# Strassen's products for half of h in two more chunks of a fused attention and MLP kernel, with a newer order of operations and column halves that shift the instruction stream

## The chip, the cores and the metric

The kernel runs on one core of a Trainium2 chip (trn2). The metric is device time in microseconds (us) of that core; the span in a profile is some 1.8 us shorter than the time of the same execution. Every kernel here gave correct results against the reference.

## The reference

Linear attention with a cosine weighting, 8 batches of 8 heads, 576 positions, head size 64, followed by a two-layer MLP whose activation is h / (1 + exp(-beta h)):

```python
q_p, k_p = phi(q, cos_w, sin_w), phi(k, cos_w, sin_w)        # relu, times cos and sin
kv  = einsum('bhsf,bhsd->bhfd', k_p, v);  z = k_p.sum(axis=2)
num = einsum('bhsf,bhfd->bhsd', q_p, kv)
x   = num / (einsum('bhsf,bhf->bhs', q_p, z)[..., None] + 1e-6)   # then to (4608, 512)
h   = x @ w_in                                               # 512 -> 2048
out = (h / (1 + exp(-beta * h))) @ w_out                     # 2048 -> 512
```

## The kernel before

The 4,608 tokens go in nine chunks (0 to 8) of 512. A chunk computes h, the activation and the output products, and the attention of the next batch is woven between them. Every chunk's h has 16 tiles of 128 features. From chunk 2 on the output product uses seven products of half size in place of eight (Strassen's scheme in Winograd's form). From chunk 5 on half of the h tiles do so too, in four pairs X, Y, Z, V:

```python
def h_fast(c, jt0, banks):                      # one pair of h tiles: 7 products, 2 matmuls of 256 columns each
    "1": prod(b_ps, w(0, 0), x(0, 0), ...)      # "5" needs t1, "6" t2, "7" t3, "4" t4: the sums of x
    "5": prod(e_ps, s1, t1, ...)                # s1..s4: the sums of the weights (wh_sums)
    ...
def wh_sums(jt):                                # 4 subtractions or additions on DVE, 128x256
def x_sums(c):                                  # 4 on DVE, 128x512

def num_mm(b, n, jp, bank, slot):               # 8 matmuls 64x65; a batch's numerator is 144 of them in one go
...
FAST = 5
for c in range(2, NTC):                         # chunks below FAST: plain h, then the output products
    x, y = o_fast(c, 0, xb, cols[0]), o_fast(c, 1, yb, cols[1])
    if c >= FAST:
        chunk(c, b, x, y, parts)                # follows a list of operations, ORDER
        continue
    sums = h_first(c)                           # 16 plain tiles
    for t, bank in enumerate(parts): num_all(b, t, bank)     # the numerator's burst
    for i, n in enumerate("156273"):            # output products, with the divisions x_part between them
        ...
        x_part(b, i, parts[i])                  # part 0 frees bank 6, which product "2" writes
```

A "numerator burst" below is that run of 144 tiny matmuls and 144 weight loads between a chunk's h and its output products.

## Time and profile before

| | before |
|---|---|
| time, median of the first 3 runs | 282.33 us (280.57 to 282.58) |
| span of the profiled run | 279.65 us, clock 1.000 |
| TensorE (PE) busy | 272.2 us, 97% |
| DVE / ACT / GpSimd busy | 209.1 / 177.8 / 71.9 us |
| matmul instructions | 3,592 records on the chip |

Read it from PE: it is busy nearly all the time, so what counts is the work in its queue and the few places where it stops. The prediction below shows those places. A table of stretches by chunk gives the scale. The columns are stretch, its length, and then each engine's busy time with its number of instructions, the granted clock, the DMA share and GB/s. The stretches run from the first output product of one chunk to that of the next, for chunks 2 to 6:

```profile
98.22:127.64 29.42, 28.94 (x396) 19.51 (x392) 17.17 (x48) 19.93 (x37) 9.01 (x10) 1.00 0.85 214
127.64:156.40 28.76, 28.76 (x403) 19.43 (x392) 21.81 (x69) 19.93 (x37) 9.06 (x10) 1.00 0.83 203
156.40:184.90 28.50, 28.15 (x425) 21.82 (x416) 22.40 (x60) 21.50 (x46) 9.06 (x10) 1.00 0.66 163
184.90:213.10 28.20, 28.20 (x497) 24.74 (x483) 22.84 (x61) 21.23 (x46) 8.94 (x10) 1.00 0.30 61
```

The last stretch holds a Strassen h (chunk 6), the first two plain ones (chunks 3 and 4). The stretches get shorter by tenths, not by microseconds.

### The profile page before, as it was taken

How to read it: one execution, taken by the hardware profiler on the slowest of the kernel's cores; microseconds unless marked ns; L12 is line 12 of the kernel's file. 1: busy time of each engine (PE TensorE's matmuls, PEld its weight loads, DVE VectorE, ACT ScalarE, POOL GpSimd, SP SyncE). 2: the span in 40 equal slices, each digit the busy share in tenths (PEclk: the TensorE clock that was granted, in tenths of full speed). 3: DMA queues.
4: the chain of work that ended last, by engine and by line, in shares of the span. 5: the costliest groups of instructions: out<-in, count | busy, mean ns of one | idle time of the engine just before them, and what ended most of it. 6: DMA issues, size and time to landing. Idle time of an engine off the chain costs nothing.

```text
span 279.6 us, 8687 instructions
## 1 busy us (share of the span) xinstructions
PE 272.2 (97%) x3592; PEld 192.4 (69%) x3592; DVE 209.1 (75%) x539; ACT 177.8 (64%) x348; POOL 71.9 (26%) x89
## 2 busy tenths in 40 slices
PE   8999999999999999999999999999999999999993
PEld 8564455455674588548854886679888886888783
DVE  5989967669999586357749977799679779649832
ACT  5778756772137557675757585896685179529911
POOL 1444000633194074106320542007400140000000
PEclk9999999999999999999999999999999999999999
DMA  7999999999979959992899289407400540033006
GB/s 243 373 394 385 391 390 323 348 244 397 164 233 330 293 151 249 182 340 41 196 193 374 61 205 250 177 12 115 116 1 7 122 113 1 2 79 74 0 2 150
DMA packets 50583, 53.98 MB, mean 193 GB/s; under 512 B 31200, under 2 KB 31472, under 8 KB 50544
## 3 DMA queue, kind: packets, MB, share of 16 engines
q1 hardware_dynamic: 47584, 45.82, 58.0%
q0 software_dynamic: 2688, 7.34, 9.2%
q8 instruction: 28, 0.46, 0.7%
q10 hardware_dynamic: 272, 0.27, 0.4%
q14 instruction: 11, 0.09, 0.2%
HBM read 36.71 MB, written 9.44 MB: 165 GB/s over the span
## 4 chain that ended last, share of the span: by engine, by line
PE 89%; DMA 5%; DVE 3%; issue 1%; ACT 0%; ACTq 0%
PE ps L544 30%; PE ps L378 22%; PE ps L472 11%; PE ps L521 8%; PE ps L426 7%; DMA raw_q<-in_q_dram 5%; PE ps L293 4%; PE ps L272 3%; PE ps L602 1%; PE ps L234 1%; PE ps L606 1%; DVE xs L315 1%; DVE vb L219 0%; PE ps L616 0%; PE ps L352 0%
## 5 line engine op out<-in xcount | busy, mean ns | idle before, releaser
L378 PE MATMUL ps<-xt,win 128*128 128x512 bf16 (+1 forms) x324 | 71.1, 377 | 0.1
L386 ACT ACTIVATE g_t<-ps,beta 128x512 bf16<-128x512 f32 x80 | 54.6, 688 | 19.2 <-PE ps L378 17.9
L378 PEld LDWEIGHTS <-win 128*128 128x128 bf16 x324 | 31.1, 98 | 35.4 <-issue 0.2
L514 POOL DMA_DIRECT2D out_dram<-o_sb x56 | 32.7, 590 | 66.6 <-DVE o_sb L595 34.3
L544 PEld LDWEIGHTS <-S 128*128 128x128 bf16 x469 | 44.2, 98 | 4.8
L417 ACT ACTIVATE g_t<-ps,beta 128x512 bf16<-128x512 f32 x64 | 41.2, 696 | 3.4 <-PE ps L426 2.2
L544 PEld LDWEIGHTS <-g_t 128*128 128x128 bf16 x357 | 32.9, 98 | 3.7
L222 POOL TENSOR_TENSOR qs<-qt,tanr 128x1152 bf16<-128x1152 bf16 x8 | 18.9, 2387 | 48.5 <-DVE S L397 17.6
L397 DVE TENSOR_TENSOR S<-g_t 128x512 bf16<-128x512 bf16 (+1 forms) x62 | 22.3, 393 | 11.5 <-ACT g_t L386 9.1
L521 PE MATMUL ps<-wout,g_t 128*128 128x512 bf16 (+1 forms) x158 | 29.2, 339 | 0.0
L544 PE MATMUL ps<-wout,g_t 128*128 128x256 bf16 (+1 forms) x231 | 28.1, 270 | 0.0
L544 PE MATMUL ps<-wout,S 128*128 128x256 bf16 (+1 forms) x238 | 27.4, 266 | 0.0
L544 PE MATMUL ps<-T,S 128*128 128x256 bf16 (+1 forms) x231 | 27.1, 269 | 0.0
L426 PE MATMUL ps<-xt,win 128*128 128x512 bf16 (+1 forms) x120 | 24.0, 336 | 0.0
L315 DVE TENSOR_TENSOR xs<-ps,rden 128x768 bf16<-128x768 f32 (+4 forms) x26 | 22.8, 883 | 0.8
L219 DVE TENSOR_SCALAR vb<-raw_v,cos 128x256 bf16<-128x256 f32 x63 | 22.9, 421 | 0.2 <-DMA raw_v<-in_v_dram 0.2
L521 PEld LDWEIGHTS <-g_t 128*128 128x128 bf16 x158 | 15.0, 98 | 11.0
L217 ACT ACTIVATE vb<-raw_v,sin 128x256 bf16<-128x256 f32 (+1 forms) x50 | 21.8, 499 | 0.8 <-DMA raw_v<-in_v_dram 0.8
L472 PE MATMUL ps<-w_stage 128*128 128x256 bf16 x120 | 20.3, 273 | 0.4 <-DVE w_stage L458 0.4
L472 PEld LDWEIGHTS <-w_stage 128*128 128x128 bf16 x160 | 15.5, 98 | 4.2 <-issue 0.5
L222 POOL TENSOR_TENSOR w_stage<-qt,tanr 128x1152 bf16<-128x1152 bf16 x4 | 9.5, 2380 | 26.1 <-DVE den L304 26.1
L426 PEld LDWEIGHTS <-win 128*128 128x128 bf16 x120 | 11.7, 98 | 6.3
(104 smaller groups left out, 384.9 us busy)
## 6 DMA issues: line engine op xcount, KB each, us to landing
raw_v<-in_v_dram SPq DMA_DIRECT2D x7, 1152.0 KB, 10.9
raw_k<-in_k_dram SPq DMA_DIRECT2D x7, 1152.0 KB, 8.4
raw_q<-in_q_dram SPq DMA_DIRECT2D x7, 1152.0 KB, 7.8
out_dram<-o_sb POOLq DMA_DIRECT2D x56, 128.0 KB, 5.2
w_stage<-in_moe_w_in_dram SPq DMA_DIRECT2D x3, 1024.0 KB, 13.3
w_stage<-in_moe_w_out_dram SPq DMA_DIRECT2D x2, 1024.0 KB, 8.4
w_stage<-in_moe_w_out_dram SPq DMA_DIRECT2D x4, 512.0 KB, 12.0
out_dram<-o_sb SPq DMA_DIRECT2D x13, 128.0 KB, 2.4
```

The costliest lines, as they stand in the source:

```text
L219: nc.vector.tensor_scalar(o, a, scalar1=t[:, n : n + 1], scalar2=None, op0=ALU.mult)
L222: return eng.tensor_tensor(dst.rearrange("q n (g p) -> q n g p", g=2), src.rearrange("q n (g p) -> q n g p", g=2), tanr[:, n0:n1].unsqueez ...
L315: nc.vector.tensor_tensor(o.rearrange("q j n s d -> q j (n s) d"), nv[:, :, a:z, :, 0:D].rearrange("q j n s d -> q j (n s) d"), rden[:, :, ...
L378: nc.tensor.matmul(ps[:, h_bank(c, jt), blocks.start * 64 : blocks.stop * 64], lhsT=win[jt // 4][:, mi, (jt % 4) * P : (jt % 4 + 1) * P], ...
L386: nc.scalar.activation(gs[c, jt // 4][:, jt % 4], ps[:, h_bank(c, jt)], AF.Silu, scale=beta[:, jt : jt + 1])
L397: return nc.vector.tensor_tensor(o, l, r, op=op)
L417: nc.scalar.activation(gs[c, jt // 4][:, jt % 4], ps[:, bank], AF.Silu, scale=beta[:, jt : jt + 1])
L426: nc.tensor.matmul(ps[:, bank, o * 64 : z * 64], lhsT=win[jt // 4][:, mi, (jt % 4) * P : (jt % 4 + 1) * P], rhs=xt[:, o:z, jp, g * HP : (g ...
L472: nc.tensor.matmul(dst, lhsT=left[:, g], rhs=right[:, :, g * HP : (g + 1) * HP], start=start and g == 0, stop=stop and g == 1, skip_group_ ...
L514: eng.dma_start(out=out_v[bb, n][:, m0:m1], in_=o_sb[hf * HP : (hf + 1) * HP, m0:m1])
L521: nc.tensor.matmul(o_ps[:, m0 : m0 + w], lhsT=gs[c, jt // 4][:, jt % 4, tt * P : (tt + 1) * P], rhs=wout[:, jt, m0 : m0 + w], start=(jt == ...
L544: nc.tensor.matmul(dst[:, m : m + w], lhsT=left(i), rhs=right[:, i, m : m + w], start=start and i == 0, stop=stop and i == order[-1], skip ...
```

## The change

Its intent: Strassen's products for half of h already from chunk 3, with a newer order of operations in those chunks, the weight sums of the four pairs moved into chunk 2 (those of the last chunk's two further pairs into chunk 6), and matmuls split in two column halves at chosen places. A split does the same work with two instructions more (a weight load and a matmul), so it moves all later instructions of PE's stream. The core of the diff:

```diff
-    def h_mm(c, jt, mis=range(4), blocks=slice(0, NB)):
+    def h_mm(c, jt, mis=range(4), blocks=slice(0, NB), cols=1):      # cols=2: two halves
...
-            o_part(1, (slot - 16) // 4, slot % 4, 2 if slot > 23 else 1)
+            o_part(1, (slot - 16) // 4, slot % 4, 2 if slot > 18 else 1)
...
-    H_COLS, O_COLS = {6: 8}, {5: ("4", "25734")}
+    SPLITS = {2: (6, 9), 3: (8, 10), 4: (7, 10), 5: (5, 0)}   # chunk: h tiles in halves, last output products in halves
...
-            if c == FAST - 1 and slot in (2, 4, 6, 8, 10, 12):
-                wh_sums((0, 4, 8, 12, 2, 6)[slot // 2 - 1])
+            if slot in (10, 12, 14):
+                for jt in ((0, 4), (8,), (12,))[slot // 2 - 5]:
+                    wh_sums(jt)
...
-    FAST = 5
+    FAST = 3
...
     (in the output products of the last plain chunk)
-        v_half(b + 1, 0, 0, 3)
+        v_half(b + 1, 0, 0, 5)
         y["5"]()
         y["c5"]()
+        if c == FAST - 1:
+            x_sums(c + 1)
...
-    ORDER = ("Y1 c1Y X5 X1 ... p3 q0 sp4 ... cuV q1 p5 ...
+    ORDER = ("p0 Y1 X1 c1X ... oy6 w8 q0 q1 cuy ...          (another order; q0, q1 far later)
```

## The prediction

> **What bounds the kernel now.** I read the page's busy shares first, then PE's own waits, the timeline around each of them, and a table of stretches by chunk.
>
> ```profile
> PE 272.2 (97%) x3592; PEld 192.4 (69%) x3592; DVE 209.1 (75%) x539; ACT 177.8 (64%) x348; POOL 71.9 (26%) x89
> ...
> PEclk9999999999999999999999999999999999999999
> ...
> PE ps L602 <- DVE zero_b L149: 1.0, 1, 1.0
> PE ps L293 <- issue: 0.9, 2, 0.5
> PE ps L293 <- ACT kv L282: 0.5, 1, 0.5
> PE ps L472 <- DVE w_stage L458: 0.4, 1, 0.4
> PE ps L234 <- DVE qb L194: 0.2, 1, 0.2
> ```
>
> TensorE is busy 97% at full clock and its listed waits come to 3.0 us: only fewer columns, or those few waits, can shorten the span of 279.6 us. The starts of successive matmuls lie 216 ns apart at 512 columns, 109 ns at 256 and 55 to 56 ns at 128 (medians over the trace). Two of the waits concern this change. The "issue" wait:
>
> ```profile
> 97.42 0.22 PE L293 MATMUL ps<-kv,qt 64*64 64x65 bf16 x4
> 98.06 0.23 PE L293 MATMUL ps<-kv,qs 64*64 64x65 bf16 x4 [0.43 <-issue]
> ...
> 126.72 0.22 PE L293 MATMUL ps<-kv,qt 64*64 64x65 bf16 x3
> 127.42 0.19 PE L293 MATMUL ps<-kv,qt 64*64 64x65 bf16 x1 [0.48 <-issue]
> ```
>
> The attention numerator is a burst of 144 tiny matmuls with 144 weight loads, 288 instructions in about 1.27 us. In chunk 2 (96.24 to 98.07) and chunk 3 (125.61 to 127.52) it takes 1.83 and 1.91 us from first to last start; in chunks 4 and 6 it takes 1.24 and 1.30. The excess is 1.20 us. Counted in PE's own stream, the two gaps stand at instructions 2755 and 3522, 767 apart, which is three blocks of 256 less one. The queue of instruction fetches moved 28 packets of 16 KB for PE's roughly 7,200 instructions, one per 256. Those fetches start at 95.50 and 125.01 us, 2.4 to 2.6 us before the gap ends. So I read a gap as PE reaching the end of a block before the next has arrived. The second wait, at L472, is chunk 5's first Strassen product behind the sums of x:
>
> ```profile
> 168.64 0.38 PE L472 MATMUL ps<-xt,win 128*128 128x256 bf16 x2
> ...
> 168.90 0.42 DVE L458 TENSOR_TENSOR w_stage<-xt 128x512 bf16<-128x512 bf16 x1
> ...
> 169.37 0.38 PE L472 MATMUL ps<-w_stage 128*128 128x256 bf16 x2 [0.35 <-DVE w_stage L458]
> ```
>
> Start to start it costs 0.5 us more than the 0.22 that two products need.
>
> [...]
>
> **The change part by part.** *Strassen in chunks 3 and 4.* Eight pairs more. A pair of plain tiles is 8 matmuls of 512 columns, 8 x 216 = 1.728 us; by products it is 14 of 256, 14 x 109 = 1.526. Eight pairs save 1.62 us of PE, on the path. ACT and DVE get four pairs' copies and adds more per chunk, about 6.8 us on DVE (16 x 0.42) and 3.0 on ACT (8 x 0.38). Chunk 5 already runs so, with 22.4 us of DVE and 21.6 of ACT in 28.6, and PE stood only in the wait above. I take chunks 3 and 4 to be like it: no new wait.
>
> *Column halves.* The built program has 3,871 matmuls against 3,589. Strassen makes 8 x (14 - 8) = 48 of the 282, so 234 are net splits at about 2.5 ns: 0.59 us lost. As a check, chunk 5's output products before ran 154 matmuls in 12.44 us where chunk 7's 112 took 12.33: 42 splits, 0.11 us, 2.6 ns each. What they are for shows when the block ends are counted in both built streams. Within the 288 instructions, the later block end of chunks 2 to 6 lay before at place 280, 263, 246, 181, 240, and lies after at 206, 223, 232, 253, 188. Two of those before stalled, at 280 and 263; none did at 246 or below, beyond 0.06 at 240. [...] I expect both gaps to go, 1.20 us, and something between 0 and 0.5 to appear in chunk 5 at 253, where I interpolate 0.2 us.
>
> *Sums of x placed earlier.* The first Strassen chunk's sums of x now stand inside the second half of chunk 2's output products, some 4 us ahead of their use: the 0.5 us wait goes.
>
> *Sums of the weights.* Four of the six, 16 operations at about 0.23 us of pitch (0.93 for four in the timeline of chunk 4), move from chunk 4 into the last third of chunk 2's h. This is the part that I distrust. DVE there before:
>
> ```profile
> 91.94 0.70 DVE L284 CAST kv<-ps 128x520 bf16<-128x520 f32 x1 [1.34 <-PE ps L272]
> 93.61 0.76 DVE L397 TENSOR_TENSOR S<-g_t 128x512 bf16<-128x512 bf16 x2 [0.97 <-ACT g_t L386]
> ...
> 98.01 0.16 DVE L304 TENSOR_TENSOR den<-ps,eps 128x12 f32<-128x12 f32 x1
> ...
> 100.85 1.04 PE L544 MATMUL ps<-wout,g_t 128*128 128x256 bf16 x8
> ```
>
> After the cast at 91.94 DVE idles 0.97, 0.17 and 0.70 us, 1.84 in all, and the new sums need 16 x 0.23 = 3.7. Laid end to end: eight sums to 94.4, the g sums to 95.9, four to 96.9, g sums to 97.9, four to 98.9, the last g sums to 99.85, then the first division (1.42 us) to 101.27 in place of 99.43. That division frees bank 6, which output product 2 must write. Product 2 began at 100.85, and without the fetch gap would begin at 100.25: PE then waits about 1.05 us. Later adds run late too, and I give 0.1 to product 4 of the second half. Cost 1.15 us.
>
> Sum: 1.62 + 1.20 + 0.5 gained, 0.59 + 1.15 + 0.2 lost, net 1.4 us.
>
> **The rivals.** (a) *DVE keeps up in chunk 2*, because PE is itself later or the sums run tighter: net 2.5 us, time near 279.5. For it: chunk 4 took 24 such operations without a PE wait. Against it: chunk 4 spread them over seven slots and had no k, v and q work in its h; chunk 2 has 13.6 us of DVE work in 16.95 already. (b) *Chunks 3 and 4 stand on new waits*, since their DMA queues are fuller: the mean DMA share is 0.85 and 0.82 in the stretches of chunks 2 and 3 against 0.66 in chunk 4's, and the transposes of x must land before the sums of x. For it: the transposes of q take 11.4 us to land (median). Against it: no wait of PE on a DMA is listed after the start, and the new order puts the q work after the x transposes. It would eat 0.5 to 2 us: 281 to 283. (c) *The fetch gaps only move*, to other blocks or to chunk 5, since the fetch's own time varies from 0.9 to 1.8 us in the trace: then only Strassen less splits is left, 1.0 us, and with the DVE wait nothing: near 282. Against it: none of the places after is above 253.
>
> **Range and chances.** From the median of 282.33 the net 1.4 gives 280.9; from the mean of the three runs (281.83), 280.4. The runs spread by 2.0 us, so I predict 280.4. Rival (a) with the lowest run of before leads to 278.4, rivals (b) and (c) to 282.4. For 2% it would have to gain 5.6 us, more than all waits and the Strassen gain together (4.6), so faster by 2% has 0.02, slower by 2% 0.02, and within it 0.96.
>
> **What would show it.** Right: matmul count up by 282; no "issue" wait above 0.3 us in the bursts of chunks 2 and 3; no wait on the sums of x at a first Strassen product; a PE wait on DVE of about a microsecond before product 2 in chunk 2, with DVE unbroken from the kv cast on; chunks 3 and 4 near 28.1 us each with PE never idle. Wrong: PE idle in chunks 3 or 4 behind ACT, DVE or a transpose; a gap in chunk 5's burst above 0.5; or no PE wait in chunk 2 at all, which gives rival (a).

## The result, and the profile after

The changed kernel took 285.31 us (median of 6 runs, 284.55 to 286.5), the kernel before 282.17 beside it (6 runs, 280.57 to 283.04). The ratio is 1.012, with a 95% interval from 1.0081 to 1.0159. Ratios are the mean time of one kernel's fast runs over that of the other's of the same rounds, so they are not quite the ratio of the medians. Executions over 1.5% slower than the fastest of the same kernel are left out of the means. The change is slower by 1.2%; 280.4 with a range of 278.4 to 282.4 had been predicted. Within 2% it is "same", but the loss is clear of the noise and has the wrong sign.

The page after, busy shares and granted clock:

```profile
PE 272.2 (96%) x3874; PEld 207.0 (73%) x3874; DVE 219.9 (78%) x571; ACT 179.5 (63%) x364; POOL 71.3 (25%) x89
...
PEclk9999999999999999997999999999999999999999
```

PE is busy as long as before, for less work, and one of the 40 slices has a lower clock. PE's own waits, longest in total first (total, times, longest):

```profile
PE ps L293 <- issue: 3.3, 2, 2.8
...
PE ps L552 <- DVE xs L315: 0.7, 1, 0.7
```

The wait on the sums of x is gone. A wait on the division is there, as predicted. The "issue" wait, which was to go, has more than tripled, and one wait alone is 2.8 us. PE's timeline in chunk 3's burst:

```profile
126.57 0.22 PE L293 MATMUL ps<-kv,w_stage 64*64 64x65 bf16 x3
129.57 0.21 PE L293 MATMUL ps<-kv,w_stage 64*64 64x65 bf16 x1 [2.78 <-issue]
```

It stands at instruction 3778 of PE's stream, 256 after 3522, where the second gap of before stood. It is a block end again, at place 223 of the burst. The table of stretches after, for the same chunks as before, and below it a short stretch just behind the wait:

```profile
97.95:130.16 32.21, 28.75 (x511) 25.26 (x503) 26.63 (x75) 21.73 (x46) 10.48 (x11) 0.98 0.93 199
130.16:160.17 30.01, 29.52 (x515) 25.44 (x508) 21.21 (x58) 21.07 (x45) 7.92 (x10) 0.96 0.78 198
160.17:188.36 28.19, 28.19 (x510) 24.21 (x501) 22.57 (x62) 20.39 (x45) 9.28 (x10) 1.00 0.68 165
188.36:216.35 27.99, 27.99 (x427) 21.79 (x417) 21.98 (x62) 21.00 (x46) 8.99 (x10) 1.00 0.28 61
...
130.16:132.50 2.34, 2.34 (x19) 1.65 (x13) 1.36 (x3) 0.41 (x2) 2.34 (x2) 0.51 0.82 108
```

Chunk by chunk the difference of 3.2 us in span adds up:

| stretch | before | after | difference | what it is made of |
|---|---|---|---|---|
| up to chunk 2's first output product | 98.22 | 97.95 | -0.27 | chunk 2's gap gone (-0.6), start and splits (+0.3) |
| chunk 2's output, chunk 3's h and burst | 29.42 | 32.21 | +2.79 | burst gap 2.91 in place of 0.64 (+2.27), half clock in the rest of the burst (+0.2), PE waits for the division (+0.85), 87 splits (+0.22), Strassen (-0.81) |
| chunk 3's output, chunk 4's h and burst | 28.76 | 30.01 | +1.25 | half clock (about +1.2), a burst gap of 0.62 that before did not have, 91 splits (+0.23), Strassen (-0.81) |
| chunk 4's output, chunk 5's h and burst | 28.50 | 28.19 | -0.31 | wait on the sums of x gone (-0.5), splits (+0.2) |
| chunk 5's output, chunk 6's h and burst | 28.20 | 27.99 | -0.21 | the splits of before are gone |
| the rest | 66.55 | 66.50 | -0.05 | |

The parts in the last column are start-to-start spacings beyond the usual 109 or 216 ns, 8 matmuls at 216 less 14 at 109 ns for a pair, and 2.5 ns a split (the mean pitches in the trace of before, twice 109.1 less 215.8 ns, give 2.4). They meet the differences within 0.1 us. The half clock is recorded from 129.06 us for 3.41 us. Products that follow each other every 109 ns elsewhere are then 213 ns apart. Five of the six runs of the changed kernel show a mean clock of 0.991 to 0.994; one shows 1.000 with 284.55, hardly shorter, so that one lost its time in another way; it has no trace here.

So the loss is in the instruction fetch. The trace records each fetch as one 16 KB packet in queue 8 (28 packets before, 30 in the change). In the table below, "block before entered" is when PE executes the first instruction of the block before, and I count from there, as if the fetch were requested then. The trace records no request, and in the first two rows the fetch starts 0.8 and 0.6 us earlier than that. The rows of runs that are told later are included, since the last column is the point:

| where | block before entered | fetch starts | gap ends | start to use |
|---|---|---|---|---|
| before, chunk 2's burst | 96.33 | 95.50 | 98.06 | 2.56 |
| before, chunk 3's burst | 125.62 | 125.01 | 127.42 | 2.41 |
| the change, chunk 3's burst | 123.55 | 127.07 | 129.57 | 2.50 |
| the change, chunk 4's burst | 156.17 | 157.44 | 159.82 | 2.37 |
| before with the bursts moved (e4), chunk 2 | 92.48 | 97.71 | 100.25 | 2.54 |
| loads in quarters (e5), chunk 3 | 123.43 | 124.72 | 127.18 | 2.46 |
| early places (e9), behind chunk 4's burst | 153.29 | 156.93 | 159.31 | 2.38 |

From start to use it takes 2.4 to 2.6 us in these seven. What varies in them is the time to its start, from 0.8 us before the block before is entered to 5.2 us after it. The DMA records show what was moving meanwhile. In the changed kernel, the raw loads of q and v (512 packets each) begin to flow at about 123.5 us, and the fetch starts at 127.07, when 476 of the first load's 512 packets have started. In the kernel before, chunk 3's fetch starts when 504 of the second load's 512 have. That suggested the theory for the experiments: **a fetch that is requested during a bulk transfer starts when that transfer is nearly done.** It was an estimate of mine from these fetches; nothing in the traces shows why a fetch should wait so.

### The profile page after: what moved, and what is told of

It is laid out like the page before. It is cut to its first block, busy times and chain, and to the rows that moved or that the text cites.

```text
span 282.9 us, 9280 instructions
## 1 busy us (share of the span) xinstructions
PE 272.2 (96%) x3874; PEld 207.0 (73%) x3874; DVE 219.9 (78%) x571; ACT 179.5 (63%) x364; POOL 71.3 (25%) x89
## 3 DMA queue, kind: packets, MB, share of 16 engines
q0 software_dynamic: 2688, 7.34, 10.6%
## 4 chain that ended last, share of the span: by engine, by line
PE 82%; DMA 9%; DVE 6%; issue 2%; SPq 1%; ACTq 0%; ACT 0%
PE ps L552 30%; PE ps L474 15%; PE ps L428 12%; PE ps L380 10%; PE ps L523 7%; DMA raw_q<-in_q_dram 5%; PE ps L293 3%; DMA raw_v<-in_v_dram 3%; PE ps L272 2%; DVE S L399 1%; DVE xs L315 1%; SPq L79 1%; PE ps L234 0%; PE ps L352 0%; DVE w_stage L454 0%
## 5 line engine op out<-in xcount | busy, mean ns | idle before, releaser
L419 ACT ACTIVATE g_t<-ps,beta 128x512 bf16<-128x512 f32 x96 | 61.1, 698 | 2.9 <-DVE ps L504 2.8
L552 PEld LDWEIGHTS <-S 128*128 128x128 bf16 x553 | 45.8, 98 | 4.2
L380 PE MATMUL ps<-xt,win 128*128 128x512 bf16 (+1 forms) x214 | 42.8, 357 | 0.1
L428 PE MATMUL ps<-xt,win 128*128 128x256 bf16 (+1 forms) x220 | 40.9, 321 | 0.0
L388 ACT ACTIVATE g_t<-ps,beta 128x512 bf16<-128x512 f32 x48 | 32.6, 689 | 10.5 <-PE ps L380 9.9
L552 PEld LDWEIGHTS <-g_t 128*128 128x128 bf16 x434 | 34.5, 99 | 4.0 <-issue 0.9
L380 PEld LDWEIGHTS <-win 128*128 128x128 bf16 x214 | 20.6, 98 | 19.3 <-issue 0.2
L552 PE MATMUL ps<-wout,g_t 128*128 128x256 bf16 (+1 forms) x280 | 28.7, 255 | 0.7 <-DVE xs L315 0.7
L523 PE MATMUL ps<-wout,g_t 128*128 128x256 bf16 (+1 forms) x177 | 29.3, 320 | 0.0
L428 PEld LDWEIGHTS <-win 128*128 128x128 bf16 x220 | 21.4, 98 | 9.3
L474 PE MATMUL ps<-w_stage 128*128 128x256 bf16 x168 | 26.5, 273 | 0.0
L474 PEld LDWEIGHTS <-w_stage 128*128 128x128 bf16 x224 | 21.6, 98 | 5.2
L523 PEld LDWEIGHTS <-g_t 128*128 128x128 bf16 x177 | 16.9, 98 | 9.2
L474 PE MATMUL ps<-xt,win 128*128 128x256 bf16 x112 | 19.1, 273 | 0.0
```

The lines of the kernel that those rows point to most:

```text
L380: nc.tensor.matmul(ps[:, h_bank(c, jt), i * 64 : (i + w) * 64], lhsT=win[jt // 4][:, mi, (jt % 4) * P : (jt % 4 + 1) * P], rhs=xt[:, i : i ...
L388: nc.scalar.activation(gs[c, jt // 4][:, jt % 4], ps[:, h_bank(c, jt)], AF.Silu, scale=beta[:, jt : jt + 1])
L419: nc.scalar.activation(gs[c, jt // 4][:, jt % 4], ps[:, bank], AF.Silu, scale=beta[:, jt : jt + 1])
L428: nc.tensor.matmul(ps[:, bank, o * 64 : z * 64], lhsT=win[jt // 4][:, mi, (jt % 4) * P : (jt % 4 + 1) * P], rhs=xt[:, o:z, jp, g * HP : (g ...
L474: nc.tensor.matmul(dst, lhsT=left[:, g], rhs=right[:, :, g * HP : (g + 1) * HP], start=start and g == 0, stop=stop and g == 1, skip_group_ ...
L523: nc.tensor.matmul(o_ps[:, m0 : m0 + w], lhsT=gs[c, jt // 4][:, jt % 4, tt * P : (tt + 1) * P], rhs=wout[:, jt, m0 : m0 + w], start=(jt == ...
```

## The experiments

Every run is compared with the kernel before on the same chip. Differences in time are against the changed kernel's 285.31, which was measured in another call, or the kernel before's median of the same call. Medians are over all runs (e1, e3, e6 and e9 each have one slow run). Traces are of one execution each. Four runs each, six in the later ones.

### e1: one raw load later in the program

```diff
-        if b + 1 < B and b != 3:
+        if b + 1 < B and b not in (3, 5):      # not the raw q of batch 6 here
             load_raw(b + 1, "q")
...
                     num_all(b, t, bank)
+                if c == FAST:
+                    load_raw(b + 2, "q")       # but behind chunk 3's burst in the program
```

> The changed kernel, with one load moved: the raw q of batch 6 (1.15 MB), issued just before chunk 3's numerator burst in the changed kernel, is issued after that burst. PE's instruction stream is the same, so every block end stays at the same place (223 in chunk 3). Theory (bulk loads in flight hold back the instruction fetch): the load traffic ends some 3 us earlier, the fetch for chunk 3's burst starts near 124 to 125.5 us in place of 127.07, the 2.8 us issue wait falls to 1 us or less, the clock stays 1.000, and the time falls by 2.5 to 4 us against the changed kernel, to 281 to 282.5. Rival (the place in the burst alone decides): the wait stays at 2.8 us, the clock at 0.994, the time near 285.3.

Measured: 286.25 us (282.97 to 287.25), ratio 1.010 (1.0023 to 1.0177). The fetch for chunk 3's burst started at 127.36, the gap was 3.39 us, and 6.8 us of half clock followed. By its wording the theory lost. But the edit did not do what it was meant to do: SyncE, which issues the loads, doesn't wait for PE's burst, and the trace has the two loads flow from 123.3 to 132.1 us as before, only in the other order. The run says nothing on a later load. Nor do all its executions lose the time alike: the one at 282.97 has a mean clock of 0.999. It does show one thing: with the loads in the other order the fetch started again near the end of the first (485 of 512 packets).

### e2: the bursts moved by 70 more instructions

```diff
-    SPLITS = {2: (6, 9), 3: (8, 10), 4: (7, 10), 5: (5, 0)}
+    SPLITS = {2: (6, 14), 3: (8, 10), 4: (7, 10), 5: (5, 0)}
```

> The changed kernel with all 14 output products of chunk 2 split in column halves in place of 9: 35 matmuls, 70 instructions more ahead of the later bursts, 0.09 us. The block ends of the bursts of chunks 3 to 6 move from 223, 232, 253, 188 to 153, 162, 183, 118; all loads stay. Theory (a fetch arrives late because it was asked for while bulk loads were queued): the fetch is asked for about 5 us earlier, before the raw loads flow, and arrives in time or under 1 us late: 281 to 282.5. Rival (whatever is asked during that stretch waits until the loads are done at 128.7 us): the wait stays near 2.8 us or grows, and the time stays near 285.3.

Measured: 281.33 us (279.87 to 283.09), ratio 0.9967 (0.9913 to 1.0021). No burst shows an issue wait, and no half clock follows one. Thirty-five more splits made the kernel 4 us faster, so it isn't the number of splits that cost, but where the block ends lie in time. The fetch for chunk 3's burst was no prompter than in the change: it started at 125.45, 4.4 us after its block before was entered (3.5 in the change). But that block was entered 7.0 us before the next was needed, at 121.01 for 128.03, in place of 3.1 us (123.55 for 126.60). It wasn't free: PE stopped for 1.28 us in chunk 3's h, exactly where a block begins whose fetch, started at 114.64 among the q transposes, took 4.26 us in place of the usual 1.0.

```profile
121.01 0.38 PE L474 MATMUL ps<-w_stage 128*128 128x256 bf16 x2 [1.12 <-ACT g_t L419]
```

The profile puts this stop down to an activation on ACT, which ended at 120.73, 0.28 us before PE went on; where PE waited for the division in the changed kernel, it went on 0.05 us after it (101.37 to 101.42). The fetch is the likelier cause, but it isn't settled.

### e3: the weight sums of chunk 2 on GpSimd

```diff
-            if slot in (10, 12, 14):
-                for jt in ((0, 4), (8,), (12,))[slot // 2 - 5]:
-                    wh_sums(jt)
+            if slot in (2, 4, 6, 8):
+                wh_sums((0, 4, 8, 12)[slot // 2 - 1], nc.gpsimd)
```

> The changed kernel with the 16 weight sums of chunk 2 taken from DVE to GpSimd, in slots 2 to 8. Theory (DVE is over its time in chunk 2's h, makes PE wait 0.7 to 0.85 us at output product 2, and makes the q work and with it the raw loads 2.4 to 2.8 us late, which brings them into chunk 3's burst): PE's wait on the division goes, the raw q and v loads are issued about 2.5 us earlier relative to before, and the issue wait in chunk 3 falls below 1.5 us with the clock at 1.000: 280.5 to 282.5. Rival (the loads meet the burst anyway, since Strassen and the missing gap bring the burst forward by 1.6 us): only the 0.85 us comes back, 284 to 285, with an issue wait of 2 us or more. Third: [...] DVE operations in chunk 2's h get longer, nothing is won.

Measured: 287.12 us (284.79 to 291.18), ratio 1.0169 (1.0088 to 1.0251). The third theory holds. DVE in the changed kernel and in this one, the same nine operations without and with the sums on GpSimd:

```profile
83.32 2.44 DVE L219 TENSOR_SCALAR vb<-raw_v,sin 128x256 bf16<-128x256 f32 x9
```

```profile
83.34 5.24 DVE L219 TENSOR_SCALAR vb<-raw_v,sin 128x256 bf16<-128x256 f32 x9
```

They take twice as long, DVE falls behind, and PE waited 2.9 us for the kv cast. The trace shows the slowing, 5.24 against 2.44 us, and not its cause: two of the nine were long before GpSimd's first sum is recorded (85.59 us). The run doesn't settle what DVE's load does to the raw loads.

### e4: the kernel before, bursts moved

```diff
-            o_part(1, (slot - 16) // 4, slot % 4, 2 if slot > 23 else 1)
+            o_part(1, (slot - 16) // 4, slot % 4, 2 if slot > 15 else 1)
```

> The kernel before, with column halves in chunk 1's output from its slot 16 on rather than from 24: 30 matmuls more, 0.08 us. The block ends of the bursts in chunks 2 to 6 move from 280, 263, 246, 181, 240 to 220, 203, 186, 121, 180. No load is moved. Theory (a late place is harmful, but load traffic decides how far the fetch lags): both issue gaps (1.2 us in all) go or shrink, time 0.6 to 1.2 us below before. Rival (the gaps belong to the loads only): the gaps stay within 0.3 us, time as before.

Measured: 281.17 us (280.54 to 284.52), ratio 0.9983 (0.9915 to 1.005). Three runs of four were at 280.54 to 281.47, about 1.4 us below the median of before; over all four the ratio shows no difference. The profiled one was at 284.52: in chunk 2, at place 220, the fetch started 5.2 us after its block before was entered, with a wait of 2.4 us and 3.4 us of half clock behind it. That start, 97.71, lies 0.5 us after the last packet of a raw load (97.17). Chunk 3 had no gap. So the very thing that hit the changed kernel also hits the kernel before when its block end lies at 220, now and then. A place alone doesn't protect. My rule, that places up to 246 are safe, was read from bursts whose fetches had happened to be served soon.

### e5: every raw load in four transfers

```diff
-        js = slice(j0, j1)
-        nc.sync.dma_start(...[:, js] ...)
+        step = 1 if b > 3 else j1 - j0
+        for a in range(j0, j1, step):
+            js = slice(a, a + step)
+            nc.sync.dma_start(...[:, js] ...)
```

> The changed kernel with every raw load from batch 4 on issued as four transfers of 288 KB in place of one of 1.15 MB; PE's stream is the same. What the first runs show: an instruction fetch that is asked for during a bulk transfer starts when that transfer ends (in the traces so far mostly at 476 to 512 of a load's 512 packets, or as a transpose ends), and the block is in use 2.4 to 2.6 us after that start. Theory A (the fetch waits for the one transfer in progress on its engine): with transfers a quarter as long, the fetch for chunk 3's burst starts within 1 us of being asked for or of the q transpose's end, near 124.5 us, the issue wait there falls below 0.8 us and no half clock follows: 281 to 283. Theory B (it waits for all that is queued, or for a fixed number of packets): its start stays at 126.5 or later, issue wait 2 us or more, 284.5 to 286.

Measured: 281.94 us (281.41 to 283.48), ratio 1.0028 (0.9988 to 1.0067): by the medians 3.4 us faster than the change with the same stream on PE, by the ratios to before (1.012 and 1.0028) some 2.6 us. Chunk 3's fetch started at 124.72, 1.3 us after its block before was entered (3.5 in the change), and PE's longest issue wait was 0.6 us:

```profile
PE ps L295 <- issue: 1.6, 3, 0.6
```

No half clock followed. Theory A holds in what it said of the wait and the time, and nearly in the start (1.3 us after the request, for within 1). One reservation: the quarters also began to flow earlier, at 117.9 in place of 123.5 us, mixed with the q transposes. The run therefore shows that the transfers decide, and fits the length of one transfer, but doesn't separate length from time.

### e6: Strassen in chunk 4 alone, in the old order

```diff
-    FAST = 5
+    FAST = 4
```
(with the sums of x placed as in the change and the split of e4.)

> The kernel before in its old order with Strassen in chunk 4 added (weight sums in chunk 3's h, where DVE has room), the sums of x placed early as in the change, and the bursts moved to 220, 203, 138, 73, 132 by column halves in chunk 1's output from slot 16. Theory (the parts add: 0.8 us from one Strassen chunk, 0.5 from the x sums, 1.2 from the two gaps, less 0.08): 279.5 to 280.5, with no PE wait on DVE before output product 2 in chunks 2 and 3. Rival (a fetch meets the raw loads in chunk 2 or 3, as in one of four runs of the moved bursts): 281.5 to 284 in some runs, with an issue wait of 2 us or more.

Measured: 286.43 us (284.88 to 290.44), ratio 1.016 (1.0105 to 1.0215). The sum of parts failed, and not only by the rival. Chunk 2's fetch was late again (2.0 us of issue wait). A new wait of 2.4 us came in chunk 4, of PE on a DVE add, with a half clock behind it as behind the first. DVE had stood 2.90 us before the raw q there; the next run shows the same at full length.

### e7: the old order in the changed kernel

ORDER of before in the kernel of e2; nothing else.

> The run with place 153, with the old order of operations in the Strassen chunks in place of the newer one. Theory (the order matters only through where the q transpose and the raw loads of chunks 3 and 4 fall; PE is never short of work in either): within 1 us of the run with place 153 (281.3), PE idle differing only in the fetch and at the first products. Rival (the newer order is what makes chunks 3 and 4 fit under their transfers): 2 us or more slower, with PE waits on DVE or ACT in chunks 3 and 4.

Measured: 299.55 us (298.0 to 300.69), ratio 1.0641 (1.0593 to 1.0689), 18 us slower than e2. My theory that the order hardly matters is wrong and the rival right. DVE and PE in chunk 3, from the timeline:

```profile
128.49 0.76 DVE L194 TENSOR_SCALAR qb<-raw_q 128x1152 bf16<-128x1152 f32 x1 [7.84 <-DMA raw_q<-in_q_dram]
...
129.64 0.37 PE L474 MATMUL ps<-w_stage,win 128*128 128x256 bf16 x1 [7.34 <-DVE ps L503]
```

The old order asks for the q work of the batch after next early in the chunk. In chunks 5 and 6 there is no such batch, so it did no harm there. In chunk 3 its raw q is still on the way, DVE stands before it for 7.84 us with the adds of the Strassen pairs behind it, and PE stands 7.34 us behind those. Chunk 4 repeats it. The newer order is what lets the two further chunks run without these waits. That is also why e6 failed in chunk 4.

### e8: the changed kernel without added column halves

```diff
-    SPLITS = {2: (6, 9), 3: (8, 10), 4: (7, 10), 5: (5, 0)}
+    SPLITS = {}
```
(and slot > 23 again in chunk 1's output.)

> The changed kernel without any added column halves (300 matmuls fewer); the block ends lie at 280, 215, 150, 85, 276 in chunks 2 to 6. Theory (the splits cost 2.5 ns each, and only the place and the loads decide about gaps): 0.75 us of splits saved; a gap in chunk 2 (280) of 0.5 to 2.5 us, in chunk 3 (215) like the changed kernel's 2.8 us if its fetch still meets the raw loads, none in chunk 4 (150), under 1 us in chunk 6 (276, little traffic): 283 to 286. Rival (the splits are what made it slow): below 281.

Measured: 281.3 us (280.41 to 281.68), ratio 0.9986 (0.9952 to 1.002). The expectation was too high: the gaps were 0.18 us in chunk 2, 1.12 in chunk 3 and 1.45 in chunk 6, and no half clock followed (mean clock 1.000). The rival's number (below 281) was just missed, but its direction is right: **without the column halves the change is 4 us faster.** In the profiled spans (282.85 and 279.84 us) the 300 matmuls, at 2.5 ns each, account for 0.75 us of 3.0, and shorter gaps and the missing half clock for some 2.2. Here chunk 3's fetch started at 124.84, just as the second raw load began (packet 23).

### e9: few halves, early places

```diff
-            o_part(1, (slot - 16) // 4, slot % 4, 2 if slot > 18 else 1)
+            o_part(1, (slot - 16) // 4, slot % 4, 2 if slot > 15 else 1)
...
-    SPLITS = {2: (6, 9), 3: (8, 10), 4: (7, 10), 5: (5, 0)}
+    SPLITS = {2: (6, 0), 4: (0, 5)}
```

> The changed kernel with 217 matmuls fewer in column halves, chosen so that the later block end of every burst lies early: 184, 119, 54, 175, 110 in chunks 2 to 6. Loads as in the change. Theory (an early place lets the fetch be asked for several us before its burst, and the splits themselves cost 2.5 ns each): no issue wait above 0.5 us in chunks 3 to 6, perhaps 0.3 in chunk 2; 0.55 us of splits saved against the change; PE's wait on the division before output product 2 stays at 0.5 to 0.7 us: 279.5 to 281, faster than the kernel before by 0.3 to 0.8%. Rival (the late fetches then stop the ordinary stream in place of the burst, as once in the run with place 153): a stop of 1 us or more outside a burst, and 281 or more.

Measured: 282.55 us (280.01 to 285.64), ratio 1.0031 (0.9981 to 1.008). No burst stopped by more than 0.3 us, but the rival is right. PE stopped in the output products behind chunk 4's burst:

```profile
155.36 0.49 PE L552 MATMUL ps<-T,S 128*128 128x256 bf16 x3
159.31 0.60 PE L552 MATMUL ps<-T,S 128*128 128x256 bf16 x2 [3.46 <-issue]
```

At place 54 the block that begins inside the burst is used up 256 instructions later, and 234 of these are burst, spent in 1 us. The next block end is reached 22 instructions behind the burst, and its fetch started only when 447 of a raw load's 512 packets had. A half clock followed. Three runs were at 280 to 281.3, three at 283.8 to 285.6.

### e10 and e11: the same with quarters, then one weight sum later

```diff
+        step = 1 if b > 1 else j1 - j0          # e10: quarters from batch 2 on
...
-            if slot in (10, 12, 14):             # e11: wh_sums(12) from slot 14
-                for jt in ((0, 4), (8,), (12,))[slot // 2 - 5]:
+            if slot in (10, 12):
+                for jt in ((0, 4), (8,))[slot // 2 - 5]:
...
         v_half(b + 1, 0, 7, 9)
+        wh_sums(12)                              # e11: to the end of chunk 2's output products
```

> The run before this one (few halves, early places) with every raw load from batch 2 on in four transfers. Theory: the two cures meet the same loss, so this wins at most 0.5 us over the one above, mainly a smaller spread: 279.3 to 280.5, highest of its runs within 1.5 us of the lowest. Rival (the four times as many transfers cost SyncE or the queue more than they give): 0.5 us or more slower than the one above, with DVE or ACT waiting longer for raw k, q or v.

> The run above with the weight sums of pair 12 moved from slot 14 of chunk 2's h to the end of its output products. Theory (DVE is 0.93 us late at the first division because of these four operations): PE's 0.5 to 0.7 us wait before output product 2 falls below 0.1, the time falls by 0.4 to 0.7 us. Rival (DVE is only late elsewhere then): PE waits on DVE at the first products of chunk 3, time as above.

Measured: e10 281.01 us (280.05 to 281.35), ratio 0.9991 (0.9968 to 1.0015). The six runs lie within 1.3 us, where e9's lay within 5.6, and the stop behind chunk 4's burst is 1.15 us in place of 3.6: the quarters cap the long waits. The time lies above its text (279.3 to 280.5). The gain over e9 in the median, 1.5 us, was larger than the text's 0.5, because e9's long stops had not been expected; in the ratios it isn't clear of the noise.

e11 280.16 us (279.74 to 282.87), ratio 0.9988 (0.9952 to 1.0024). PE's wait on the division, 0.35 us beyond the usual spacing in e10, is no longer among its waits, and no wait on DVE took its place in chunk 3. This part of the theory holds; the time against e10 is inconclusive, 0.85 us in the medians, nothing in the ratios (one run had 282.87).

### e12: the kernel before with loads in quarters

The edit of e10 in the kernel before.

> The kernel before with the raw loads from batch 2 on in four transfers; PE's stream and every place as before (280 and 263 in chunks 2 and 3). Theory (at these places the fetch is asked for inside the burst or just ahead of it, so the 2.4 to 2.6 us from start to use show even with no traffic): the gaps of 0.56 and 0.64 us stay within 0.3 us, time within 0.6 us of before. Rival (before's gaps were the loads' doing): both gaps go, 1.2 us faster.

Measured: 281.82 us (281.23 to 283.29), ratio 1.0033 (1.0002 to 1.0064): no gain, if anything a loss of 0.3%. Chunk 2's gap, at place 280, grew to 1.41 us. Chunk 3's, at 263, was gone: its fetch started at 124.18, 2.2 us before its block before was entered. So neither text is right in full. In chunk 2 the fetch started inside the burst (96.32 us, the burst at 96.15), and its 2.5 us to use show with the loads in quarters too. Short transfers are no cure for a bad place.

### e13 and e14: room on both sides of each block end

```diff
-    SPLITS = {2: (6, 9), 3: (8, 10), 4: (7, 10), 5: (5, 0)}
+    SPLITS = {2: (6, 0), 3: (0, 9), 5: (0, 10)}
```
(with slot > 15 in chunk 1's output and wh_sums(12) as in e11; e13 with quarters, e14 with whole loads.)

> As the run with one weight sum later (loads in quarters, 12's sums moved), with the column halves laid out anew: later block ends at 184, 119, 184, 120, 171 in chunks 2 to 6, 119 matmuls fewer than the change. Theory (a block end needs several us of ordinary matmuls both ahead of it, from the block before, and behind it, to the next one; place 54 in chunk 4 left only 22 instructions after the burst, and PE stopped 0.6 to 3.5 us there): no issue wait above 0.3 us anywhere, 278.8 to 279.8, 0.4 to 0.8% faster than the kernel before, and a spread under 1.5 us. Rival (with this traffic some fetch is always late, only elsewhere): an issue wait of 0.6 us or more at another place, 280 or more.

> As the run above with whole raw loads of 1.15 MB. Theory (with room on both sides the fetch can wait for a whole load and still be in time): within 0.5 us of the run above. Rival (the room of some 6 to 7 us is not enough for a load that follows a transpose): some runs 2 us slower, with an issue wait of 1 us or more and a half clock behind it.

Measured: e13 280.29 us (278.82 to 280.47), ratio 0.9937 (0.9908 to 0.9965). e14 279.28 us (278.74 to 280.85), ratio 0.9915 (0.9887 to 0.9943), the kernel before at 282.22. e13's median and its spread of 1.65 us lie above their text (278.8 to 279.8, under 1.5), and e14 was 1.0 us faster, not within 0.5; between the two the ratios don't decide. PE's waits in e14:

```profile
PE ps L610 <- DVE zero_b L149: 1.0, 1, 1.0
...
PE ps L293 <- issue: 0.3, 1, 0.3
```

The first is at the start of the kernel. After 100 us, that is from chunk 2's output products on, PE has no wait in the list at all. What is left is 0.3 us in chunk 2's burst at place 184 (0.4 in e13, a little above its text). Both are faster than both kernels, and e14, which is the simpler one, is the version to take: 0.85% below the kernel before and, by the two ratios, 2.0% below the change. Whole loads did no harm here, so the rival of e14 fell: with room on both sides a late fetch was still in time. There is little to spare: in e13, chunk 4's fetch started 4.1 us after its block before was entered (147.85) and took 2.5 to use, of 6.6 us that it had.

## Why the prediction was wrong

**The step that failed** is in the part on the column halves: "Two of those before stalled, at 280 and 263; none did at 246 or below, beyond 0.06 at 240", and from it "I expect both gaps to go, 1.20 us". The places were counted correctly, the reading of a gap as a block that comes too late was right, and the gap of chunk 2 at 206 did go. But the place did not fix when a fetch started. At 223 and 232 the fetches started 3.5 and 1.3 us after their blocks before were entered, and cost 2.9 and 0.6 us. The long one was followed by 3.4 us of half clock, about 1.2 us more. Against the expected 1.20 us gained at chunks 2 and 3, chunk 2 gained 0.6 and chunk 3 lost 2.3; with the 0.6 in chunk 4 and the half clock this term is 4.7 us from its forecast. The whole error is 4.6 (3.2 lost for 1.4 gained). I had the sign of danger in hand: rival (c) says that the fetch's own time varies from 0.9 to 1.8 us. I looked at how long the packets took and not at how late they started, and thought the rival worth no more than the loss of the gain.

**Strassen in chunks 3 and 4.** Right. h of chunk 3, from its first plain matmul to the burst, took 14.43 us in place of 15.15, h of chunk 4 14.41 in place of 15.16: 0.7 us each, with 24 and 21 splits (0.06) in it, for 0.81 less splits foreseen. That PE gets no new wait there was right only because of the newer order, which I had judged from PE's and DMA's side alone; e7 shows 7.1 to 7.3 us of waiting in each of the two chunks without it.

**Column halves' cost.** Right within what can be read: 0.2 us for some 90 of them in each stretch.

**Sums of x.** Right: the wait is gone and the stretch is 0.31 us shorter, with 0.2 of splits in it.

**Weight sums on DVE in chunk 2.** Right, mechanism and size: DVE ran unbroken from the kv cast, the first division ended at 101.37 us (worked out: 101.27), and PE waited before product 2:

```profile
100.41 0.96 DVE L315 TENSOR_TENSOR xs<-ps,rden 128x768 bf16<-128x768 f32 x1
```

```profile
101.42 0.81 PE L552 MATMUL ps<-wout,g_t 128*128 128x256 bf16 x6 [0.69 <-DVE xs L315]
```

The wait is 0.85 us from start to start, for 1.05 foreseen. e11 confirms it by moving four of the operations away.

**Chunk 5's burst.** I gave 0.2 us at place 253; it had 0.03. That burst meets little traffic (a DMA share of 0.02 from 186.5 to 188.36 us). The latest place was harmless and an earlier one cost 2.9 us, which is the short form of what went wrong.

**What stays open.** The raw loads came 5 us later in the changed kernel than before, relative to chunk 3's burst (first raw q packet 123.5 against 118.5 us, with the burst at 125.6 in both). DVE's lag in chunk 2 was my reason for that, since the q transposes wait for DVE; e3 was to test it and spoiled it, as DVE was slower there (5.24 for 2.44 us). It isn't shown, and it is doubtful: at the first division DVE was 1.9 us later than before (101.37 against 99.43), and in e8 and e9, with the same sums on DVE, the loads began at 120.8 and 117.1 us. Nor is it shown whether the fetch waits for one transfer or for a number of packets: e5 changed length and time together. Nor is "nearly done" a rule: e2's fetch for chunk 3's burst started at packet 215 of the first load's 512, e4's at 334, the latter 0.8 us after its block before was entered. The occasional long wait in e4 was seen in one execution of four and not taken apart.

## What to carry to other kernels

Here dense bursts of tiny matmuls ate instructions faster than they were fetched (288 in 1.25 us, against 2.4 us or more for a block of 256), so the place of the 256-instruction block ends in PE's stream matters, and so does the bulk traffic when the block before is entered (with the loads in quarters chunk 3's wait was at most 0.6 us, for 2.8). Give each block end several microseconds of ordinary matmuls ahead of it and behind it (6.6 us were just enough in e13, 3.1 too few in the change), and count both sides. Don't tune a place on a few quiet executions, and when work moves an early operation onto a transfer still in flight, look at which engine will stand in front of it.

## What the runs show of the fetch and the clock

- In bursts of 288 instructions in 1.25 us and just behind one, PE stood 0.2 to 3.6 us in these runs, in waits that the profile lists as issue. From the start of a fetch to use it was 2.4 to 2.6 us in all seven gaps of the table.
- The kernel before has 28 fetches for some 7,200 instructions, one per 256 or so. In its chunk 2 the fetch started 286 instructions before the gap; in the change's chunk 3 it started at 127.07 us, and PE had needed the block from 126.60 on.
- PE's 28 blocks are in queue 8 of the trace of before, with 11 other instruction packets in queue 14 (30 and 12 in the change). A fetch started up to 5.2 us after its block before was entered, often at 447 to 504 of a load's 512 packets. What held it until then is not shown.
- In the change 3.41 us of half clock followed 3.41 us (125.65 to 129.06) of which PE's records cover 1.14, a third. The length of one wait doesn't decide: 6.8 us of half clock followed e1's gap of 3.39 us and 3.4 us followed e4's wait of 2.4, but none followed e3's wait of 2.9 (mean clock 0.998). What decides is not shown.
